# Moving the weight-conversion steps of an attention, experts and gate kernel off the expert changes

## The chip, the cores and the metric

The kernel runs on one core of one Trainium2 chip. The metric is the device time of one execution in microseconds. The core has five engines that run their own instruction queues in order: TensorE (PE, matmuls), VectorE (DVE), ScalarE (ACT), GpSimd (POOL) and SyncE (SP, which issues nearly all DMA transfers here). An engine that waits for a semaphore holds everything behind it in its queue.

## The reference

Banded attention, then a mixture of four experts, then a gated network whose output projection follows directly:

```python
x = attention(q, k, v)                       # (1536, 512)
p = domain_probs / (domain_probs.sum(-1, keepdims=True) + 1e-09)
for e in range(4):
    h = np.maximum(x @ w1[e], 0.0)           # (1536, 1024)
    out += p[:, e:e + 1] * (h @ w2[e])       # (1536, 512)
a = out @ moe2_w1
b = out @ moe2_w2
h = (a * b) @ w3
result = h @ w_out
```

The last four weights arrive as 64-bit floats. The kernel turns them into 32-bit floats itself, piece by piece, on the engines that are not TensorE.

## The kernel before

**Numbers.** Every float32 matrix is held as a sum of two parts, "h" and "l", and each product is three matmuls (`three`, lines 60 to 62: high by high, high by low, low by high). `split` (lines 54 and 55) makes the parts: ACT casts the high part, DVE or POOL subtracts to get the low one.

**Chunks and stages.** The 1536 tokens are three chunks of 512. After the attention, chunk 0 goes through all four experts alone: 32 items n = 0 to 31, each one hidden block of 128 rows (an "up" product) and, two items later, its share of the second product (a "down", 12 matmuls into the four PSUM tiles o0 to o3). Then chunks 1 and 2 go through the experts in reverse order in 16 pair steps n = 0 to 15, four for each expert. A pair step makes two hidden blocks for two chunks with seven half-size products instead of eight (Strassen's scheme, `Pairs.run`), whose sums are DVE additions from PSUM (line 735). The products share four PSUM tiles z. Pair steps 4, 8 and 12 change expert: they also run the last two downs of chunk 1 and all eight of chunk 2 of the expert before, in four lists `downs[0]` to `downs[3]` that stand between the products. At the end of a chunk's downs DVE multiplies o0 to o3 by the probabilities (line 836 for the first expert, 839 for later ones, after which POOL adds to `acc`, line 840), and the next down can't write o0 until DVE has read it. After pair step 15 the ten downs of the last expert follow ("the ends"), while the weights that the next stage needs are loaded and split into the slots. The gate stage then makes the product of the last two weights (`w34`, j = 0 to 7, each 24 matmuls) and after that the gate itself.

**The order of work** is written out by hand: `tc.manual_schedule` keeps every engine's queue in program order.

**Conversion steps.** `Convert.step` is called 43 times at places listed by hand. There are 40 pieces of 128 x 512. One step in the middle of the run does five things: ACT takes the absolute value of a piece that has landed (line 541) and POOL clamps it (line 543); SP stores the piece that the step before finished (line 571); DVE runs four instructions on the piece that the step before began (lines 550 to 553); POOL adds (line 554); and SP loads a further piece (line 580), which waits until DVE has read the buffer that it goes to. The 41st and 42nd step load nothing, and the 43rd call finds nothing to do. The places are `CONVERTS` (after item n of chunk 0), `INSIDE` (in pair step n, between the ACT relu and the DVE subtraction of one output), `BETWEEN` (in pair step n, list j, after its down m) and `ENDS` (after one of the ten last downs).

**Others that the change touches.** `XSUMS` are the items n of chunk 0 after which a part of the sums of x for the pair steps (t1 to t4) is made. `last_x(c, d)` (lines 844 and 845) turns a quarter of `acc[c]` into the high part on ACT and the low part on POOL; all twelve calls stand between the ends and the gate stage. The buffers of the conversion (`cpool`) are allocated behind those of the pair steps (`xp`, `tpool`) and given back with them before `w34` takes its place.

Of the kernel before, what the change touches and what calls it, by code (L numbers as in the profile page):

```python
# [27 lines left out]
KC, FC = DM // P, F // P  # L28
CW = 512
NCH = N // CW  # L30
# [5 lines left out]
FILL = (6, 4)  # L36
W_TILE = 4
LAG = 2
XSUMS = (21, 23, 24, 26, 27, 28)
CONVERTS = (4, 6, 7, 8, 10, 11, 12, 13, 14, 18, 20, 22)  # L40
ENDS = (2, 4, 6)
BETWEEN = [(4, 3, 0)] + [(n, j, m) for n in (4, 8, 12) for j, m in ((0, 0), (1, 0), (1, 1), (2, 0), (2, 1))]
INSIDE = [(n, 1, 1) for n in range(15) if n not in (4, 8, 12)]
BIG = 1.0e30
MASKED = -1.0e9

# [5 lines left out]
def split(nc, hi, lo, src, lo_engine=None):  # L52

    nc.scalar.copy(hi, src)  # L54
    (lo_engine or nc.vector).tensor_tensor(lo, src, hi.bitcast(F32), op=ALU.subtract)  # L55


def three(nc, out, wh, wl, xh, xl, start, stop):

    nc.tensor.matmul(out, wh, xh, start=start, stop=False)  # L60
    nc.tensor.matmul(out, wh, xl, start=False, stop=False)  # L61
    nc.tensor.matmul(out, wl, xh, start=False, stop=stop)  # L62
# [712 lines left out]
def experts_and_gate(tc, g, x_hi, x_lo, slots, experts, first_time):  # L775

    nc = tc.nc
    name = "" if first_time else "g"
    with ExitStack() as ctx:
# [2 lines left out]
        ps_z = ctx.enter_context(tc.tile_pool(name=name + "ps_z", bufs=4, space=PSUM))  # L782
        ps_a = ctx.enter_context(tc.tile_pool(name=name + "ps_a", bufs=1, space=PSUM))
        acc = [big.tile([P, KC, CW], F32, name=f"acc{c}") for c in range(NCH)]
        of_experts = ExitStack()
        xp = of_experts.enter_context(tc.tile_pool(name=name + "xp", bufs=1))
        tpool = of_experts.enter_context(tc.tile_pool(name=name + "xt", bufs=1))
        cpool = of_experts.enter_context(tc.tile_pool(name=name + "cv", bufs=2))
        ring = experts.ring
        if not first_time:  # L790
            for key in list(ring.of):
# [6 lines left out]
        def load_slot(s, src):  # L798

            raw = pool.tile([P, F], F32, name="wr")  # L800
            nc.sync.dma_start(raw, src)
            coming.append((s, raw))

        def land(keep=0):
            while len(coming) > keep:
                s, raw = coming.pop(0)
                split(nc, *slots[s], raw)

        work, pending = experts.work, experts.pending
        convert = Convert(nc, cpool, g.pieces if first_time else [])  # L810
# [5 lines left out]
        def down(e, c, f, fs=None, tail=False):  # L816
            fs = fs or list(range(FC))
            hi, lo = slots[f]
            hh, hl = pending.pop((e, c, f))
            if f == fs[0]:  # L820
                state["o"] = [
                    ps_z.tile([P, CW], F32, name="z") if tail else ps_a.tile([P, CW], F32, name=f"o{d}")
                    for d in range(KC)
                ]
            if f == fs[3]:
                state["p"] = xp.tile([P, CW], F32, name="prob")
                nc.sync.dma_start(state["p"], g.prob_dram[e, c * CW : (c + 1) * CW].partition_broadcast(P))
            o = state["o"]
            for d in range(KC):
                ds_ = slice(CW + d * P, CW + (d + 1) * P)  # L830
                three(nc, o[d], hi[:, ds_], lo[:, ds_], hh, hl, f == fs[0], f == fs[-1])
            ring.give((e, c, f))
            if f == fs[-1]:
                for d in range(KC):
                    if e == (pairs[0] if c else 0):
                        nc.vector.tensor_tensor(acc[c][:, d], o[d], state["p"], op=ALU.mult)
                        continue
                    t = tmp()
                    nc.vector.tensor_tensor(t, o[d], state["p"], op=ALU.mult)  # L839
                    nc.gpsimd.tensor_tensor(acc[c][:, d], acc[c][:, d], t, op=ALU.add)  # L840

        def last_x(c, d):

            nc.scalar.copy(x_hi[c][:, d], acc[c][:, d])
            nc.gpsimd.tensor_tensor(x_lo[c][:, d], acc[c][:, d], x_hi[c][:, d].bitcast(F32), op=ALU.subtract)
# [11 lines left out]
        def land_until(n):  # L857

            while coming and len(work) - len(todo) - len(coming) <= n:
                land(len(coming) - 1)  # L860
            load_more()
# [12 lines left out]
        for n, w in enumerate(work):  # L874
# [14 lines left out]
            if n >= LAG:  # L889
                e, c, f = work[n - LAG]  # L890
                down(e, c, f)
                if n >= FC and n % FC == LAG - 1:
                    land_until(n + FC - LAG - 1)
            if n in CONVERTS:
                convert.step()
            if n in XSUMS:
                next(xsums, None)
# [15 lines left out]
        for n in range(last + 1):  # L913
# [9 lines left out]
            def issue(j):  # L923
                for m, (e, c, f) in enumerate(downs[j]):
                    down(e, c, f, order.get(c))
                    if (n, j, m) in BETWEEN:
                        convert.step()
# [13 lines left out]
            def out(row, c, z):  # L941
# [6 lines left out]
                else:  # L948

                    to = x_hi[2][:, f - 4], x_lo[2][:, f - 4]  # L950
                experts.out((e, c, f), z, to, convert.step if (n, row, c) in INSIDE else None)

# [3 lines left out]
        for n, (e, c, f) in enumerate([w for d in ends(pairs[-1]) for w in d]):  # L956
            down(e, c, f, order[c], tail=c == 2)
            if n in ENDS:
                convert.step()
# [3 lines left out]
        split(nc, *slots[7], raws.here[0])  # L963
        raws.used()
        assert not raws.here
        for c in range(NCH):
            for d in range(KC):
                last_x(c, d)
        ring.free.remove((xp, "h3"))
        of_experts.close()  # L970

# [6 lines left out]
        for j in range(FC):  # L978
            hi, lo = slots[4 + j % 4]
            z = ps_z.tile([P, CW], F32, name="z") if j else ps_a.tile([P, CW], F32, name="o0")  # L980
            for gc in range(FC):
                oh, ol = slots[gc // 2]
                os_ = slice((gc % 2) * DM, (gc % 2 + 1) * DM)
                gs = slice(gc * P, (gc + 1) * P)
                three(nc, z, hi[:, gs], lo[:, gs], oh[:, os_], ol[:, os_], gc == 0, gc == FC - 1)
            split(nc, w34h[:, j], w34l[:, j], z)
            land()
            load_slot(4 + j % 4, g.w3t_f32[j + 4] if j < 4 else g.wab_f32[j - 4])

        def final(ps, hid, f, js, f0=0, f1=FC - 1):  # L990
            hh, hl = hid
            for j in js:
                ts = slice(j * P, (j + 1) * P)
                three(nc, ps[j], hh[:, ts], hl[:, ts], w34h[:, f], w34l[:, f], f == f0, f == f1)
# [226 lines left out]
def tile_attention_experts_gate(  # L1221
# [42 lines left out]
    slots += slot_tiles(rest, 4, FC)  # L1264

    experts_and_gate(tc, g, x_hi, x_lo, slots, experts, True)

    with tc.If(g.banded < 1):

        with tc.tile_pool(name="gn", bufs=1) as gn:  # L1270

            neg = gn.tile([P, 4], F32, name="neg")
            nc.vector.tensor_scalar(neg, wf, 0.0, 2.0**32, op0=ALU.is_lt, op1=ALU.mult)
            nc.vector.tensor_add(neg, neg, wf)
            full = gn.tile([P, 2], F32, name="full")
            for j in range(2):
                nc.vector.scalar_tensor_tensor(
                    full[:, j : j + 1], wf[:, 2 * j + 1 : 2 * j + 2], 2.0**32, neg[:, 2 * j : 2 * j + 1],
                    op0=ALU.mult, op1=ALU.add,
                )  # L1280

            nc.vector.tensor_scalar(full[:, 1:2], full[:, 1:2], -1024.0, None, op0=ALU.max)
            g.ng, g.nl = full[:, 0:1], full[:, 1:2]
            general_attention(tc, g, x_hi, x_lo)
        experts_and_gate(tc, g, x_hi, x_lo, slots, experts, False)
# [50 lines left out]
```

## Time and profile before

| | us |
|---|---|
| median of 3 runs | 832.39 |
| lowest and highest | 831.73, 832.85 |
| the profiled execution | 831.13 |
| its span, first to last instruction | 829.3 |
| PE busy in it | 805.5 (97%) |
| DVE, POOL, ACT busy | 615.0, 382.2, 315.0 |

The profile is one execution. Matmuls of 512 columns are shown 389 ns long but start one every 0.226 us where nothing holds them (46.00 us for 204 of them in a stretch without a wait), so a busy PE is a PE whose shown matmuls overlap. A row of the timeline ends with the idle time of the engine in front of the instruction and what ended it.

### The profile page before, as it was taken

What the parts mean: (1) busy time and instruction counts of PE and PEld (TensorE: products, weight loads), DVE (VectorE), ACT (ScalarE), POOL (GpSimd) and SP (SyncE); (2) the same over time, 40 slices, a digit from 0 to 9 for tenths busy, and PEclk for the clock granted to TensorE, in tenths of its full rate; (3) what the DMA queues carried; (4) which work ended last, traced back from release to release, by engine and by line L of the source; (5) the groups of instructions that cost most, each with busy time, mean ns of one, the idle gap of its engine ahead of it and who ended that gap; (6) DMA issues with size and microseconds to landing.
All of it is one profiled execution on the core that took longest, in us unless ns stands there. A gap on an engine that the chain in (4) does not pass through costs nothing.

```text
span 829.3 us, 11170 instructions
## 1 busy us (share of the span) xinstructions
PE 805.5 (97%) x3956; PEld 659.1 (79%) x3957; DVE 615.0 (74%) x1049; ACT 315.0 (38%) x655; POOL 382.2 (46%) x360
## 2 busy tenths in 40 slices
PE   9999999999999999899889989999999999999997
PEld 5888888888887887788677768778888888888886
DVE  8995477887829889889978988898553733888750
ACT  7996243443223342244313432333353332233210
POOL 7885032561336556554857567654291002433400
PEclk9999999999999999999999999999999999999999
DMA  9940456864202323433352344342532220201011
GB/s 274 278 123 12 151 197 208 252 187 159 71 26 64 114 94 125 163 100 117 114 202 80 113 127 148 93 134 69 171 127 97 81 72 26 97 32 51 2 44 62
DMA packets 42471, 96.52 MB, mean 116 GB/s; under 512 B 3930, under 2 KB 10122, under 8 KB 42406
## 3 DMA queue, kind: packets, MB, share of 16 engines
q1 hardware_dynamic: 41734, 95.18, 36.1%
q8 instruction: 33, 0.54, 0.3%
q10 hardware_dynamic: 672, 0.54, 0.3%
q14 instruction: 32, 0.26, 0.1%
HBM read 82.04 MB, written 13.66 MB: 115 GB/s over the span
## 4 chain that ended last, share of the span: by engine, by line
PE 64%; DVE 22%; ACT 4%; issue 4%; DMA 3%; POOL 2%; SPq 0%; DVEq 0%; ACTq 0%; POOLq 0%
PE z L60 13%; PE z L62 12%; PE z L61 12%; PE o L60 6%; PE o L62 6%; PE o L61 6%; DVE t L728 5%; DVE t L735 5%; PE sp L255 2%; DVE ca L551 2%; DVE cr L553 2%; DMA raw<-in_w_ab_dram 2%; DVE sl L55 2%; DVE ca L550 2%; PE tp L294 2%
## 5 line engine op out<-in xcount | busy, mean ns | idle before, releaser
L60 PE MATMUL z<-xh,sh 128*128 128x512 f32 x348 | 135.9, 391 | 1.4 <-DVE t L735 1.4
L62 PE MATMUL z<-xh,sl 128*128 128x512 f32 x348 | 135.5, 389 | 0.0
L61 PE MATMUL z<-xl,sh 128*128 128x512 f32 x348 | 135.5, 389 | 0.0
L543 POOL TENSOR_SCALAR ca<-ca 128x512 f32<-128x512 f32 x40 | 65.9, 1648 | 150.5 <-ACT ca L541 150.5
L55 POOL TENSOR_TENSOR sl<-wr,sh 128x512 fp32r<-128x512 f32 (+1 forms) x48 | 50.8, 1080 | 134.6 <-ACT sh L54 129.8
L55 DVE TENSOR_TENSOR sl<-wr,sh 128x1024 fp32r<-128x1024 f32 (+1 forms) x73 | 85.3, 1185 | 22.0 <-ACT sh L54 21.6
L54 ACT CAST sh<-wr 128x1024 fp32r<-128x1024 f32 (+2 forms) x121 | 87.0, 749 | 38.1 <-DMA wr<-in_w_moe_dram 13.7
L735 DVE TENSOR_TENSOR t<-t,z 128x512 f32<-128x512 f32 x112 | 74.7, 679 | 5.6 <-PE z L62 4.1
L60 PEld LDWEIGHTS z<-xh,sh 128*128 128x128 f32 x348 | 65.4, 188 | 16.6 <-issue 2.3
L62 PEld LDWEIGHTS z<-xh,sl 128*128 128x128 f32 x348 | 65.3, 188 | 14.3 <-DVE sl L55 0.2
L61 PEld LDWEIGHTS z<-xl,sh 128*128 128x128 f32 x348 | 65.3, 188 | 13.3
L840 POOL TENSOR_TENSOR acc<-acc,t 128x512 f32<-128x512 f32 x36 | 53.9, 1530 | 42.3 <-DVE t L839 42.3
L554 POOL TENSOR_TENSOR cr<-cr,ca 128x512 f32<-128x512 f32 x40 | 57.6, 1439 | 15.7 <-DVE cr L553 15.7
L55 POOL TENSOR_TENSOR sl<-t,sh 128x256 fp32r<-128x256 f32 (+1 forms) x48 | 53.0, 1119 | 20.6 <-ACT sh L54 20.2
L310 POOL TENSOR_TENSOR pt<-pt,r 128x232 f32<-128x232 f32 (+1 forms) x95 | 48.8, 546 | 7.6 <-DVE r L241 3.9
L541 ACT ACTIVATE ca<-raw 128x512 f32<-128x512 f32 x40 | 26.7, 668 | 63.1 <-DMA raw<-in_w_ab_dram 30.6
L60 PE MATMUL z<-sh,sh 128*128 128x512 f32 x120 | 46.7, 389 | 0.0
L61 PE MATMUL z<-sl,sh 128*128 128x512 f32 x120 | 46.7, 389 | 0.0
L62 PE MATMUL z<-sh,sl 128*128 128x512 f32 x120 | 46.7, 389 | 0.0
L281 ACT ACTIVATE pt<-t,negmax 128x232 f32<-128x232 f32 (+1 forms) x96 | 44.9, 475 | 4.0 <-DVE negmax L270 3.9
L54 ACT CAST sh<-t 128x256 fp32r<-128x256 f32 (+1 forms) x48 | 21.9, 478 | 54.4 <-DVE t L728 54.4
L624 ACT ACTIVATE xh<-t 128x512 fp32r<-128x512 f32 x24 | 15.2, 632 | 59.0 <-DVE t L735 59.0
(266 smaller groups left out, 1973.0 us busy)
## 6 DMA issues: line engine op xcount, KB each, us to landing
wr<-in_w_moe_dram SPq DMA_DIRECT2D x60, 512.0 KB, 3.6
raw<-in_w3t_dram SPq DMA_DIRECT2D x16, 512.0 KB, 4.3
raw<-in_w_ab_dram SPq DMA_DIRECT2D x16, 512.0 KB, 3.8
wr<-wab_d SPq DMA_DIRECT2D x16, 512.0 KB, 3.2
raw<-in_w_out_dram SPq DMA_DIRECT2D x8, 512.0 KB, 3.1
w3t_d<-cr SPq DMA_DIRECT2D x16, 256.0 KB, 2.4
wab_d<-cr SPq DMA_DIRECT2D x16, 256.0 KB, 4.1
wr<-w3t_d SPq DMA_DIRECT2D x8, 512.0 KB, 3.2
```

What stands on the lines that cost most here:

```text
L54: nc.scalar.copy(hi, src)
L55: (lo_engine or nc.vector).tensor_tensor(lo, src, hi.bitcast(F32), op=ALU.subtract)
L60: nc.tensor.matmul(out, wh, xh, start=start, stop=False)
L61: nc.tensor.matmul(out, wh, xl, start=False, stop=False)
L62: nc.tensor.matmul(out, wl, xh, start=False, stop=stop)
L281: nc.scalar.activation(st[u][gr][:, hh, 0:w], t[:, 0:w], AF.Exp, bias=nm, scale=-1.0, accum_out=st[u]["sums"][:, h : h + 1])
L310: nc.gpsimd.tensor_tensor(pt[:, hh, 0:w], pt[:, hh, 0:w], r[:, hh : hh + 1].to_broadcast([P, w]), op=ALU.mult)
L543: nc.gpsimd.tensor_scalar(a, a, 2.0**-15, None, op0=ALU.max)
L554: nc.gpsimd.tensor_tensor(rest, rest, a, op=ALU.add)
L728: nc.vector.tensor_tensor(out, a, b, op=op)
L735: add = lambda o, a, b: nc.vector.tensor_tensor(o, a, b, op=ALU.add)
L840: nc.gpsimd.tensor_tensor(acc[c][:, d], acc[c][:, d], t, op=ALU.add)
```

## The change

It moves conversion steps and spreads `last_x`. The number of calls stays 43, 42 of them with work.

- Chunk 0: three steps more, after items 24, 26 and 31; `XSUMS` goes from 21, 23, 24, 26, 27, 28 to 21, 23, 25, 27, 28, 29.
- Pair steps: none in pair step 0 (was one). At each expert change (pair steps 4, 8, 12) the step in list 0 and the second one in list 2 go: two less each time. Pair step 4 keeps the one in list 3.
- The ends: after downs 2 and 4 (was 2, 4 and 6, of which the last found nothing to do).
- The product `w34`: five calls, after j = 3 to 7, the last of which finds nothing to do.
- `cpool` is allocated ahead of `xp` and `tpool` and lives on through the gate stage.
- Of the twelve calls of `last_x` the four of chunk 0 stay in place; the other eight are spread over j = 0 to 6.

```diff
-XSUMS = (21, 23, 24, 26, 27, 28)
-CONVERTS = (4, 6, 7, 8, 10, 11, 12, 13, 14, 18, 20, 22)
-ENDS = (2, 4, 6)
-BETWEEN = [(4, 3, 0)] + [(n, j, m) for n in (4, 8, 12) for j, m in ((0, 0), (1, 0), (1, 1), (2, 0), (2, 1))]
-INSIDE = [(n, 1, 1) for n in range(15) if n not in (4, 8, 12)]
+XSUMS = (21, 23, 25, 27, 28, 29)
+CONVERTS = (4, 6, 7, 8, 10, 11, 12, 13, 14, 18, 20, 22, 24, 26, 31)
+W34 = (3, 4, 5, 6, 7)
+LASTX = ((0, 1), (2,), (3,), (4,), (5,), (6,), (7,), ())
+ENDS = (2, 4)
+BETWEEN = [(4, 3, 0)] + [(n, j, m) for n in (4, 8, 12) for j, m in ((1, 0), (1, 1), (2, 0))]
+INSIDE = [(n, 1, 1) for n in range(1, 15) if n % 4]
@@ experts_and_gate
+        cpool = ctx.enter_context(tc.tile_pool(name=name + "cv", bufs=2))
         of_experts = ExitStack()
         xp = of_experts.enter_context(tc.tile_pool(name=name + "xp", bufs=1))
         tpool = of_experts.enter_context(tc.tile_pool(name=name + "xt", bufs=1))
-        cpool = of_experts.enter_context(tc.tile_pool(name=name + "cv", bufs=2))
@@
-        for c in range(NCH):
-            for d in range(KC):
-                last_x(c, d)
+        for d in range(KC):
+            last_x(0, d)
@@ for j in range(FC)
             load_slot(4 + j % 4, g.w3t_f32[j + 4] if j < 4 else g.wab_f32[j - 4])
+            if j in W34:
+                convert.step()
+            for c in LASTX[j]:
+                last_x(1 + c // KC, c % KC)
```

## Rows read from the trace of the kernel before

**Rows 1.** The page, part 1: busy us (share of the span) and instructions of each engine.

```profile
PE 805.5 (97%) x3956; PEld 659.1 (79%) x3957; DVE 615.0 (74%) x1049; ACT 315.0 (38%) x655; POOL 382.2 (46%) x360
```

**Rows 2.** Waits of PE, 250 to 262 us: us in total, times, longest.

```profile
PE z L60 <- DVE t L735: 1.4, 2, 0.8
```

**Rows 3.** Waits of PE, 300 to 562 us, all of them.

```profile
PE o L60 <- DVE t L839: 7.2, 4, 2.4
PE o L60 <- DVE acc L836: 4.1, 2, 2.7
PE z L60 <- DVE t L735: 2.1, 4, 0.6
PE o L61 <- DVE h2l L627: 1.1, 1, 1.1
PE o L61 <- DVE h3l L627: 1.1, 1, 1.1
```

**Rows 4.** Windows: stretch, us, busy (instructions) by engine, PE clock, DMA share, GB/s.

```profile
300.00:560.00 260.00, 244.64 (x1061) 197.06 (x1059) 228.68 (x320) 85.82 (x162) 159.12 (x123) 1.00 0.39 127
596.00:642.00 46.00, 46.00 (x204) 38.10 (x204) 23.54 (x23) 20.43 (x30) 25.01 (x16) 1.00 0.37 120
```

**Rows 5.** Timeline of PE around its longest wait: start us, us, what.

```profile
344.37 0.39 PE L62 MATMUL z<-t2h,sl 128*128 128x512 f32 x1
347.48 0.47 PE L60 MATMUL o<-h2h,sh 128*128 128x512 f32 x1 [2.72 <-DVE acc L836]
347.78 0.39 PE L61 MATMUL o<-h2l,sh 128*128 128x512 f32 x1
```

**Rows 6.** Timeline of DVE, pair step 4, list 0.

```profile
311.18 1.42 DVE L550 TENSOR_SCALAR ca<-ca 128x512 int32<-128x512 int32 x1
...
314.53 0.69 DVE L553 SCALAR_TENSOR_TENSOR cr<-raw,cr 128x512 f32<-128x512 uint32 x1
315.14 2.48 DVE L836 TENSOR_TENSOR acc<-o,prob 128x512 f32<-128x512 f32 x4
```

**Rows 7.** Timelines of DVE and ACT, pair step 8, lists 2 and 3.

```profile
427.55 0.42 DVE L550 TENSOR_SCALAR ca<-ca 128x512 int32<-128x512 int32 x1
...
430.55 0.43 DVE L552 TENSOR_SCALAR cr<-ca 128x512 int32<-128x512 int32 x1 [0.88 <-DMA wab_d<-cr]
...
434.10 0.69 DVE L627 SCALAR_TENSOR_TENSOR h2l<-t,h2h 128x512 fp32r<-128x512 f32 x1 [1.80 <-ACT h2h L624]
...
432.88 0.66 ACT L541 ACTIVATE ca<-raw 128x512 f32<-128x512 f32 x1 [7.83 <-DMA raw<-in_w_ab_dram]
```

**Rows 8.** Timeline of DVE: the same addition in pair steps 5, 6 and 7.

```profile
361.26 0.68 DVE L735 TENSOR_TENSOR t<-t,z 128x512 f32<-128x512 f32 x1
...
377.23 0.68 DVE L735 TENSOR_TENSOR t<-t,z 128x512 f32<-128x512 f32 x1
...
393.20 0.68 DVE L735 TENSOR_TENSOR t<-t,z 128x512 f32<-128x512 f32 x1
```

**Rows 9.** Timeline of DVE ahead of pair step 0.

```profile
244.58 0.69 DVE L735 TENSOR_TENSOR t<-t,z 128x512 f32<-128x512 f32 x1 [4.13 <-PE z L62]
```

**Rows 10.** Timelines of SP's queue, DVE and PE, the ends and the first w34 products.

```profile
582.64 0.32 SPq L647 DMA_DIRECT2D wr<-wo_d  x1
...
587.60 0.37 SPq L647 DMA_DIRECT2D wr<-wo_d  x1
...
598.41 1.23 DVE L55 TENSOR_TENSOR sl<-wr,sh 128x1024 fp32r<-128x1024 f32 x1 [1.96 <-ACT sh L54]
...
601.03 0.39 PE L60 MATMUL z<-sh,sh 128*128 128x512 f32 x1
```

**Rows 11.** Timeline of DVE, w34 product j = 4 and the next.

```profile
624.56 1.84 DVE L55 TENSOR_TENSOR sl<-wr,sh 128x1024 fp32r<-128x1024 f32 x1 [0.25 <-ACT sh L54]
629.06 0.69 DVE L55 TENSOR_TENSOR w34l<-z,w34h 128x512 fp32r<-128x512 f32 x1 [2.65 <-ACT w34h L54]
```

**Rows 12.** The page, part 6: a load of the conversion, count, size, us to landing.

```profile
raw<-in_w_ab_dram SPq DMA_DIRECT2D x16, 512.0 KB, 3.8
```

## The prediction

> **What bounds the kernel now.** TensorE does: it is busy for 805.5 of 829.3 us [rows 1]. So the question is only where it isn't, and the first view is the list of its waits. Two waits, 1.4 us, lie in pair steps 0 and 1 [rows 2]. Between 300 and 562 us there are twelve, 7.2 + 4.1 + 2.1 + 1.1 + 1.1 = 15.6 us, and every one of them ends on a DVE instruction [rows 3]. Behind 562 us PE never waits; the stretch of the w34 products has it busy for 46.00 of 46.00 us [rows 4].
>
> A wait costs more than its length. The longest is shown as 2.72 us, but from the start of the matmul before it to that of the one behind it 347.48 - 344.37 = 3.11 us go by, where 46.00 / 204 = 0.2255 us is the pace [rows 4, 5]; the next start comes 0.30 us later. So the loss is 2.88 + 0.08 = 2.96 us, 0.24 more than the wait. I put 0.24 on each: the twelve lose 15.6 + 12 x 0.24 = 18.5 us. A second reading of the same stretch bounds that from above: its 1,061 matmuls needed 1,061 x 0.2255 = 239.3 of 260 us, so 20.7 us at most are lost, some of them matmuls whose records are missing [rows 4].
>
> The page "Perfetto Trace Analysis" of the Trainium skill ("Identifying the Most-Contended Engine") says that matmul busy time flatters TensorE and that the busy share of its weight loads shows the headroom. By that rule, 197.06 / 260 = 75.8% against 38.10 / 46 = 82.8% where nothing waits leaves 260 x (1 - 75.8 / 82.8) = 22.0 us and a time of 810.4 [rows 4]. The rows of the waits give 3.5 us less; I go by them, and the rule's time is rival F.
>
> DVE is late for two reasons, and a conversion step stands in both. First, at the expert changes. In list 0 of pair step 4 a step holds DVE from 311.18 to 315.14, 3.96 us, and the four readings of o0 to o3 stand right behind it, while PE wants o0 for the next down [rows 6]. In list 2 of pair step 8 the second of two steps begins at 427.55, waits 0.88 us for the store of the buffer that it writes, and its ACT part holds ACT until a load lands; the relu behind it comes late, DVE idles another 1.80 us for that, and only then come the readings of o [rows 7]. Six of the twelve waits are of this kind (11.3 us: three behind list 0, three behind list 3). Second, in the pair steps between. The same DVE addition starts at 361.26, 377.23 and 393.20, every 15.97 us [rows 8], while PE's 66 matmuls of a pair step need 66 x 0.2255 = 14.88. DVE falls 1.1 us behind in each, starts out late from the expert change, and by the third or fourth step PE waits for a z tile or for the low part of a hidden block. That makes the other six waits (4.3 us).
>
> **The change part by part.** (1) The step of list 0 goes at three changes. DVE then reads o0 to o3 right at 311.2 instead of 315.1, 3.9 us earlier, against a wait of 1.4 there: that wait goes, with 2.5 us to spare. Its siblings at the other changes are of the same make.
>
> (2) The second step of list 2 goes at three changes. In pair step 8, 427.55 to 431.6 is taken off DVE's queue, and the relu that waited behind the load is free of it, another 1.8 us [rows 7]: 5.9 us against a wait of at most 2.4. In pair step 4 the step of list 3 stays and takes some 4 us itself, but it too now stands 4 us earlier on DVE, against a wait of 2.7 [rows 3, 5]. So (1) and (2) give back 11.3 + 6 x 0.24 = 12.7 us.
>
> (3) The six waits of the pair steps: DVE comes out of each change earlier against PE, by at least the 2.5 us to spare, and gains up to 4. Three steps of 1.1 us eat 3.3 of that. In the old order the PE lost 4.3 + 6 x 0.24 = 5.7 us in two and a half expert rounds, some 2.3 a round, less than the 2.5 to 4. So these waits go as well: 5.7. Nearest to a doubt here: the margin is a microsecond or so, and the bound on the other side is that all 5.7 stay.
>
> (4) The step of pair step 0 goes. In DVE's queue it stands behind the additions that end the two waits of [rows 2] (the step belongs to the output (1, 1), made after them), so these stay (1.4 + 2 x 0.24 = 1.9 us) and nothing is gained; their cause is in the same queue (readings of o, then the sums of the weights), which the change leaves alone.
>
> (5) Three steps more in chunk 0. The one after item 31 falls on a DVE that idles 4.13 us before its next addition, the step takes 3.96 [rows 6, 9]. Those after items 24 and 26 take the place of a part of the sums of x, which moves on by an item. An item is 24 x 0.2255 = 5.4 us of PE, and its hidden block is due two items later, so 10.8 us of cover: cost 0. With the cover gone, one step, 4.0 us. A gain is excluded, since PE doesn't wait there. On SP each step's load waits for DVE, and behind it stand the first loads of the pair weights: these come up to 4 us later and are wanted a full item after that.
>
> (6) The ends. Two steps there now load (3.8 us each [rows 12]); before, none did. What stands behind them in SP's queue are the weights for the w34 products, and ACT's part of the second step waits for the load of the first, with the cast of slot 0 behind it. The tightest of these chains: the weights of the second w34 product are split by 598.41 + 1.23 = 599.64 and wanted at 601.03, 1.39 us of slack [rows 10]. On the other hand the third load of that chain went out at 587.60, 5 us behind the one before, held by the store of the very last piece [rows 10]; that store moves away. Bounds: 0, or one whole load late, 3.8 - 1.39 = 2.4. I take 0, as the loads before the slack are offset by that store.
>
> (7) The four working steps in w34 (j = 3 to 6; the call at j = 7 does nothing). DVE has 1.84 + 0.69 us of splits there in a product of 24 x 0.2255 = 5.4 [rows 11]. With 4.0 more it is 6.5, 1.1 late each, 4.4 in all; but what it splits is wanted three products later, 16.2 us. Cost 0. The eight spread calls of `last_x` run on ACT and POOL, and what they make is first read after the w34 products: cost 0, and the first casts of w34 lose eight casts ahead of them in ACT's queue, which nobody waited for: gain 0.
>
> (8) The kept buffers: `xp` and `tpool` hold what the w34 and gate tiles then overlay; `cpool` lay behind both and nothing reused it, so no wait arises: 0.
>
> Sum: 12.7 + 5.7 = 18.4, or 18.5 unrounded. The profiled execution's own time, 831.13, becomes 812.6 (its span 829.3 becomes 810.8, the 1.8 us around it stay). The median of the runs shown is 1.26 higher: 832.39 - 18.5 = 813.9.
>
> **The rivals.** A: the waits of the pair steps come back. For it: DVE's 15.97 against 14.88 stays as it is; against it: the head start of part (3). Time: 813.9 plus up to 5.7, say 817. B: the readings of o stay late at one or the other list because the steps that stay are slowed by loads and stores: the three waits behind list 3 stay, about half of 12.7, so 820.2. For it: even the steps that stay wait for loads; against it: 5.9 us off the queue for a wait of 2.4. C: the ends come 2.4 us late as in (6): 816.3. D: the steps do not matter, DVE is late through its other work, so nothing moves: 832. Against it: rows 6 show the step as the very instruction before the late one.
>
> E, slower than before: the four steps in w34 become a chain, each one's DVE part waiting for its predecessor's load. Place: ACT's in-order queue, where the absolute value waits for a load with the casts of w34 and of the slots behind it. Price at its worst: DVE 3.96, the longest that ACT stood for a load 7.83, its instruction 0.66 [rows 6, 7], the splits 2.53 [rows 11]: 15.0 a product, 9.6 over the 5.4, 38.4 in four, less the 16.2 of cover: 22.2 us, and 813.9 + 22.2 = 836.1. It decides from (18.5 + 16.2) / 4 + 5.4 = 14.1 us a product on. Against it: only two of the four steps load anything, and a step's DVE part works on the piece of the step before.
>
> One row speaks for E's direction: the same instruction took 1.42 us in rows 6 and 0.42 in rows 7. The Trainium skill's page "SBUF — State Buffer" ("Who interferes with whom") has a rule for it: DVE and GpSimd share a pair of ports, and the one that comes second stands still until the other's instruction is over. By it, steps that run beside the spread subtractions of POOL are dearer than those beside a quiet POOL; with 1.0 us on each of the four instructions, 4.0 a step, E's price without the wait for loads would be 4 x (10.5 - 5.4) = 20.4 against 16.2 of cover, 4.2 us, and a time of 818.1; that is rival G.
>
> F, more is lost than the waits show: PE's count of matmuls allows up to 20.7 us, so 811.7 without the waits of pair step 0; for it, that count; against it, records that are missing. By the page named above it would be 810.4.
>
> **How the numbers follow.** Forecast, 813.9: 0.66. A 0.12, B 0.06, C 0.05, D 0.03, E 0.04, F 0.02, G 0.02. Low: all of 20.7, 811.7, or the 1.9 of pair step 0 as well as the 18.5, 812.0; 811.5. High: all of A's 5.7, 819.6; that takes in C and G, and leaves out B, D and E, 0.13. A measurement here tells 0.2%, 1.7 us, from no change. Faster: forecast, A, B, C, F, G, 0.93; same: D, 0.03; slower: E, 0.04.
>
> **What would show it.** In the profile after: the list of PE's waits holds the two of pair steps 0 and 1 and at most one or two more; DVE's readings of o start within a microsecond of the last matmul into o at all three changes; the same addition in pair steps 5 to 7 comes nearer to 14.9 than to 15.97 us apart; PE stays busy throughout the ends, w34 and the gate. Waits on z tiles at the third pair step of a round would be A; on o behind list 3, B; a first wait at the second w34 product, C; waits in w34 from j = 7 on, E.

## The result, and the profile after

The changed kernel takes 811.79 us (median of 4 runs, 811.33 to 813.1) against 832.61 of the kernel before: a ratio of 0.9754, 95% interval 0.9737 to 0.9771. The forecast was 813.9, between 811.5 and 819.6.

| | before | after |
|---|---|---|
| profiled execution, us | 831.13 | 811.86 |
| span, us | 829.3 | 810.1 |
| PE busy, us | 805.5 (97%) | 802.1 (99%) |
| DVE, POOL, ACT busy, us | 615.0, 382.2, 315.0 | 614.9, 381.6, 315.5 |

The work of DVE, POOL and ACT is the same to within a microsecond; only where it stands has changed. PE's busy time is 3.4 us less, though it runs the same matmuls: a matmul behind a wait is shown longer (0.47 us in [rows 5], against 0.39), and late starts that are not listed as waits count as busy too. The page of after, part 1 (busy us and share of the span), and below it all waits of PE over the whole span of after (us in total, times, longest). Helper lines have moved down by two: L62 to L64 are the matmuls, L737 the additions, L838 and L841 the readings of o.

```profile
PE 802.1 (99%) x3957; PEld 661.3 (82%) x3957; DVE 614.9 (76%) x1049; ACT 315.5 (39%) x655; POOL 381.6 (47%) x360
```

```profile
PE z L62 <- DVE t L737: 1.4, 2, 0.8
PE tp L183 <- DVE warm L177: 1.2, 1, 1.2
```

The twelve waits of [rows 3] are gone, all of them, and the two of [rows 2] stand as they were. (The wait of 1.2 us is at the very start of both kernels.)

DVE in list 0 of pair step 4, after; [rows 6] are the same place before:

```profile
309.98 0.68 DVE L737 TENSOR_TENSOR t<-t,z 128x512 f32<-128x512 f32 x1
310.71 2.73 DVE L838 TENSOR_TENSOR acc<-o,prob 128x512 f32<-128x512 f32 x4
314.11 0.69 DVE L737 TENSOR_TENSOR t<-t,z 128x512 f32<-128x512 f32 x1 [0.67 <-PE z L64]
```

The four readings start at 310.71, where before they started at 315.14, and the next addition now waits 0.67 us for PE: the roles are exchanged. At the end of the same pair step the step of list 3 is still there, and the readings behind it start at 338.82 instead of 346.64. Against PE, DVE has gained 7 us there: PE's last matmul into o, 0.7 us behind the start of the readings now at 339.52, was 6.3 us ahead of it at 340.29. Before, then after:

```profile
346.64 2.48 DVE L836 TENSOR_TENSOR acc<-o,prob 128x512 f32<-128x512 f32 x4
```

```profile
338.21 0.69 DVE L555 SCALAR_TENSOR_TENSOR cr<-raw,cr 128x512 f32<-128x512 uint32 x1
338.82 2.48 DVE L838 TENSOR_TENSOR acc<-o,prob 128x512 f32<-128x512 f32 x4
```

The addition of [rows 8] in pair steps 5 and 6; in pair step 7 it starts at 386.85:

```profile
354.91 0.69 DVE L737 TENSOR_TENSOR t<-t,z 128x512 f32<-128x512 f32 x1 [0.42 <-PE z L64]
...
370.88 0.68 DVE L737 TENSOR_TENSOR t<-t,z 128x512 f32<-128x512 f32 x1
```

DVE still needs 15.97 us for a pair step, more than PE. It begins level with PE (the 0.42 us that it waits in pair step 5) and reaches the next expert change before its delay has cost PE anything.

Windows of after over the ends, the w34 products and the first gate steps (us, busy by engine, PE clock, DMA share, GB/s): PE busy without a break where the change put new work.

```profile
556.00:576.00 20.00, 20.00 (x90) 16.57 (x89) 12.82 (x13) 5.83 (x6) 9.40 (x7) 1.00 0.52 159
576.00:622.00 46.00, 46.00 (x205) 38.09 (x204) 34.95 (x37) 22.64 (x33) 33.18 (x21) 1.00 0.50 160
```

### The profile page after: what moved, and what is told of

The parts are those of the page before. It is cut to its first block, busy times and chain, and to the rows that moved or that the text cites. A ratio compares the mean times of both kernels' runs of the same rounds, so it can differ in the third digit from the quotient of the medians.

```text
span 810.1 us, 11165 instructions
## 1 busy us (share of the span) xinstructions
PE 802.1 (99%) x3957; PEld 661.3 (82%) x3957; DVE 614.9 (76%) x1049; ACT 315.5 (39%) x655; POOL 381.6 (47%) x360
## 4 chain that ended last, share of the span: by engine, by line
PE 95%; ACT 1%; DVE 1%; POOL 1%; DMA 1%; issue 0%; ACTq 0%; POOLq 0%; DVEq 0%
PE z L62 18%; PE z L64 18%; PE z L63 18%; PE o L62 12%; PE o L64 12%; PE o L63 12%; PE sp L257 2%; PE tp L296 2%; PE op L335 1%; PE op L336 1%; ACT pt L283 1%; PE sp L296 1%; DMA keys<-in_k_dram 1%; DVE t L730 1%; POOL pt L312 0%
## 5 line engine op out<-in xcount | busy, mean ns | idle before, releaser
L545 POOL TENSOR_SCALAR ca<-ca 128x512 f32<-128x512 f32 x40 | 68.2, 1706 | 155.2 <-ACT ca L543 155.2
L62 PE MATMUL z<-xh,sh 128*128 128x512 f32 x348 | 135.6, 390 | 1.4 <-DVE t L737 1.4
L64 PE MATMUL z<-xh,sl 128*128 128x512 f32 x348 | 135.5, 389 | 0.0
L57 DVE TENSOR_TENSOR sl<-wr,sh 128x1024 fp32r<-128x1024 f32 (+1 forms) x73 | 91.2, 1265 | 22.5 <-ACT sh L56 16.9
L737 DVE TENSOR_TENSOR t<-t,z 128x512 f32<-128x512 f32 x112 | 74.9, 680 | 10.2 <-PE z L64 8.7
L62 PEld LDWEIGHTS z<-xh,sh 128*128 128x128 f32 x348 | 65.3, 188 | 15.5 <-issue 1.2
L64 PEld LDWEIGHTS z<-xh,sl 128*128 128x128 f32 x348 | 65.3, 188 | 14.2 <-DVE sl L57 0.2
L842 POOL TENSOR_TENSOR acc<-acc,t 128x512 f32<-128x512 f32 x36 | 52.1, 1480 | 34.5 <-DVE t L841 34.5
L62 PE MATMUL z<-sh,sh 128*128 128x512 f32 x120 | 46.7, 389 | 0.0
L64 PE MATMUL z<-sh,sl 128*128 128x512 f32 x120 | 46.7, 389 | 0.0
```

What stands on the lines that cost most here:

```text
L545: nc.gpsimd.tensor_scalar(a, a, 2.0**-15, None, op0=ALU.max)
L737: add = lambda o, a, b: nc.vector.tensor_tensor(o, a, b, op=ALU.add)
```

## The experiments

Two theories. **P**, that of the prediction: a step costs what the reading or the deadline behind it on DVE comes late, so its place decides. **N**: what counts is the number of steps between the first and the last pair step, wherever in that stretch. All edits below are against the changed kernel, and "more than the changed kernel" compares with its median of 811.79. The kernel before, run again beside the experiments, had medians of 832.85 (the first three below and the sums of pair step 0) and 831.95 (the others), so less than a microsecond between two medians says nothing.

### The steps of list 0 back

```diff
-W34 = (3, 4, 5, 6, 7)
+W34 = (3, 4)
-... for j, m in ((1, 0), (1, 1), (2, 0))]
+... for j, m in ((0, 0), (1, 0), (1, 1), (2, 0))]
```

> The changed kernel with the step of list 0 put back at the three expert changes and three calls fewer in the w34 stage. Theory P (the place of a step counts: it costs what the readings of o behind it, or the next deadline on DVE, come late): the three waits behind list 0 come back, 4.7 us and 0.24 on each, 5.4 in all; DVE catches up in the rest of the change, so the waits of the pair steps do not come back: 811.8 + 5.4 = 817.2. Theory N (the number of steps between the first and the last pair step counts, wherever they stand): 20.8 us for seven steps moved out, 3.0 a step, so three steps give 811.8 + 9.0 = 820.8, the same as in e2_list2.

Measured: 815.58 us, ratio to the kernel before 0.9794 (0.9776 to 0.9812). Waits of PE beside the 1.4 us of pair steps 0 and 1:

```profile
PE o L62 <- DVE t L841: 2.8, 2, 1.6
...
PE o L63 <- DVE h3l L629: 0.5, 1, 0.5
```

3.8 us more than the changed kernel. Two waits behind list 0, not three: at the first expert change the step costs nothing, since DVE arrives there early enough (why, is read below from the run with the step in pair step 0). The pair steps stay almost free of waits (one of 0.5). P, at 817.2, is 1.6 too high; N, at 820.8, is off by 5.

### The second steps of list 2 back

```diff
-W34 = (3, 4, 5, 6, 7)
+W34 = (3, 4)
-... for j, m in ((1, 0), (1, 1), (2, 0))]
+... for j, m in ((1, 0), (1, 1), (2, 0), (2, 1))]
```

> The changed kernel with the second step of list 2 put back at the three expert changes and three calls fewer in the w34 stage. Theory P: the three waits behind list 3 come back (6.6 us and 0.24 on each, 7.3), and since DVE then leaves the change late, also the six waits of the pair steps (5.7): 811.8 + 13.0 = 824.8. Theory N: 820.8, as e1_list0.

Measured: 820.66 us, ratio 0.9853 (0.9835 to 0.9871), 8.9 us more than the changed kernel. Waits of PE:

```profile
PE z L62 <- DVE t L737: 3.5, 6, 0.8
PE o L62 <- DVE acc L838: 1.6, 1, 1.6
...
PE o L63 <- DVE h2l L629: 1.1, 1, 1.1
PE o L63 <- DVE h3l L629: 1.1, 1, 1.1
PE o L62 <- DVE t L841: 0.9, 1, 0.9
```

The six waits of the pair steps are all back: 3.5 less the 1.4 of pair step 0, and 1.1 twice, 4.3 us as before. Of the three behind list 3 two are back, smaller (1.6 and 0.9 against 2.7 and 2.4). The eight waits, 6.8 us and 0.24 on each, make 8.7 us; the medians lie 8.9 apart and the two profiled executions 10.3, so late starts that are not listed have a part here too. P's 824.8 is 4.1 too high, as one of its nine waits is missing and the two behind list 3 are small. The time falls on N's 820.8, but N wanted the same time for both experiments, and they lie 5.1 us apart with as many steps.

### Both back

```diff
-W34 = (3, 4, 5, 6, 7)
+W34 = ()
-... for j, m in ((1, 0), (1, 1), (2, 0))]
+... for j, m in ((0, 0), (1, 0), (1, 1), (2, 0), (2, 1))]
```

> The changed kernel with both steps put back at the three expert changes and none left in the w34 stage; only the steps of chunk 0 and of pair step 0, the buffers and the spread of last_x stay as changed. Theory P: all twelve waits, 18.5 us, 830.3. Theory N: six steps of 3.0, 829.8. If the steps of chunk 0, the buffers or the spread had given part of the gain, it would come out by that much lower.

Measured: 829.87 us, ratio 0.9964 (0.9951 to 0.9977), 18.1 us more than the changed kernel: most of the gain is given back. The time fits P (830.3) and N (829.8) alike. The two alone sum to 3.8 + 8.9 = 12.7. So the costs are not additive: each kind alone is partly paid from DVE's slack, both together are not. Of the 5.4 us between the two, some 1.5 in the trace are the clock (last section). Its waits of PE on o:

```profile
PE o L62 <- DVE t L841: 5.6, 4, 1.6
PE o L62 <- DVE acc L838: 4.1, 1, 4.1
...
PE o L63 <- DVE h3l L629: 1.1, 1, 1.1
```

In pair step 4 there was a wait of 1.36 us behind list 0 and one of 2.72 behind list 3 before, 4.08 in all [rows 3, 5]. Here the first is missing (DVE comes earlier, with no step in pair step 0; see the next experiment), and the second is 4.15: the lost time went to the next deadline on the same queue. With four waits on z tiles in the pair steps, 1.6 us, ten of the twelve waits are back, 12.4 of 15.6 us, and not all twelve, as P had it. This kernel is 3.0 us faster than the kernel before beside it (829.87 against 832.85), so that much of the gain does not hang on these six steps. What DVE has gained ahead of the first expert change is probably a part of it; the rest is not traced.

### The step after item 31 back in pair step 0

```diff
-CONVERTS = (..., 20, 22, 24, 26, 31)
-INSIDE = [(n, 1, 1) for n in range(1, 15) if n % 4]
+CONVERTS = (..., 20, 22, 24, 26)
+INSIDE = [(n, 1, 1) for n in range(15) if n % 4 or not n]
```

> The changed kernel with the step after item 31 of chunk 0 moved back into pair step 0. By part (4) of the prediction nothing comes of that step's place: the two waits of PE stay as they are (1.4 us) and the time is 811.8. Rival: the step in pair step 0 is what kept DVE late into the first expert change; then a wait of PE at list 0 or list 3 of pair step 4 shows, 1 to 3 us, up to 814.8.

Measured: 811.65 us, ratio 0.9757 (0.9741 to 0.9774). All waits of PE but that at the start of the program (1.2) and one of 0.4 on a load in the attention:

```profile
PE z L62 <- DVE t L737: 1.4, 2, 0.8
```

That step's place is worth nothing by itself, as part (4) had it. But it does move DVE: the readings in list 0 of pair step 4 start 0.2 us ahead of PE's last matmul into o with it (311.61 against 311.84) and 1.6 us without (310.71 against 312.32 in the changed kernel). Nothing waits for these 1.4 us here. But they fit the wait of 1.36 us at that place, which is there in the kernel before, with the step of pair step 0 and that of list 0, and missing in both experiments with that of list 0 alone.

### All of last_x back ahead of w34

```diff
-        for d in range(KC):
-            last_x(0, d)
+        for c in range(NCH):
+            for d in range(KC):
+                last_x(c, d)
@@ for j in range(FC)
-            for c in LASTX[j]:
-                last_x(1 + c // KC, c % KC)
```

> The changed kernel with all twelve calls of last_x back between the ends and the w34 stage. By part (7) of the prediction nothing waited for them: 811.8, no wait of PE behind 262 us. Rival: with the four conversion steps in the w34 stage the casts that stand ahead of the first w34 splits on ACT now matter, and PE waits for a z tile there: 8 casts of 0.52 us, up to 4.2 us more, 816.

Measured: 811.52 us, ratio 0.975 (0.9734 to 0.9767). Waits of PE beside those of pair step 0 and of the program's start:

```profile
PE z L62 <- DVE t L841: 0.3, 1, 0.3
```

One wait of 0.3 us shows at the second w34 product, on a z tile that DVE reads late. The time shows nothing of the spread.

### The sums of pair step 0 first

What is left are the two waits of pair steps 0 and 1. In the changed kernel DVE stands idle for 2.64 us there until the last down is done, then reads o four times, then makes the sums of the weights, and only then the additions for which PE waits. The edit uses the idle time for the sums, in pair step 0 alone:

```diff
         prep(0)
-        issue(0)
         early = n % (FC // 2) or not n
-        if early:
+        if not n:
+            prep(1)
+        issue(0)
+        if early and n:
             prep(1)
```

> The changed kernel with, in pair step 0 alone, the sums of the weights put ahead of the two downs and so ahead of the four readings of o in DVE's queue. If the two waits that are left come from DVE doing readings and sums one after the other behind the downs: DVE has 2.6 us idle there, the sums take some 4.7, so both waits (1.4 us, 1.9 with what lies around them) go or nearly go: 809.9 to 810.5, under both kernels. If they come from something else in that step (the slots that the splits write are still read by PE, and ACT and POOL wait in the middle of the sums' splits), the waits move to a later product and the time stays 811.8 or rises by what ACT stands still, up to 3 us.

Measured: 809.57 us, ratio 0.9726 (0.9709 to 0.9743), 2.2 us under the changed kernel and the fastest of all. DVE in the changed kernel, then in this one, then all waits of PE in this one but that of 1.2 us at the very start:

```profile
248.89 2.80 DVE L841 TENSOR_TENSOR t<-o,prob 128x512 f32<-128x512 f32 x4 [2.64 <-PE o L64]
...
256.16 0.68 DVE L737 TENSOR_TENSOR t<-t,z 128x512 f32<-128x512 f32 x1
```

```profile
245.68 1.37 DVE L730 TENSOR_TENSOR t<-wr 128x256 f32<-128x256 f32 x1
...
249.07 1.27 DVE L843 TENSOR_TENSOR t<-o,prob 128x512 f32<-128x512 f32 x2
...
252.18 0.68 DVE L737 TENSOR_TENSOR t<-t,z 128x512 f32<-128x512 f32 x1
```

```profile
PE sp L257 <- DMA keys<-in_k_dram: 0.6, 1, 0.6
```

The addition that PE waited for starts at 252.18; in the changed kernel at 256.16. Of the 2.3 us by which the two spans differ, 1.8 are gained here; the rest lies at the start of the program, where the edit does nothing. Behind the attention PE now waits for nothing.

### More steps in w34

Rival E put a point from which the steps in w34 would cost. Two experiments look for it. First, the three additional steps of chunk 0 out, seven calls in w34, all of them with work:

```diff
-CONVERTS = (..., 20, 22, 24, 26, 31)
-W34 = (3, 4, 5, 6, 7)
+CONVERTS = (..., 20, 22)
+W34 = (1, 2, 3, 4, 5, 6, 7)
```

> The changed kernel with the three additional steps of chunk 0 taken out and two more working steps in the w34 stage (seven calls, j = 1 to 7) so that more of them load. If the w34 stage has cover of three products for what its splits feed, 811.8 and no wait of PE there. Rival E of the prediction, a chain of load, ACT and DVE: PE waits in w34 or the gate, some 5 to 10 us.

Measured: 820.96 us, ratio 0.986 (0.9844 to 0.9876), 9.2 us more. Its waits of PE beside those of pair step 0 and of the program's start, and DVE's splits of the w34 products:

```profile
PE o L62 <- ACT h0h L56: 3.6, 1, 3.6
PE z L62 <- DVE w34l L57: 1.6, 1, 1.6
...
PE z L64 <- DVE sl L57: 0.8, 2, 0.4
```

```profile
598.21 0.68 DVE L57 TENSOR_TENSOR w34l<-z,w34h 128x512 fp32r<-128x512 f32 x1
604.52 0.68 DVE L57 TENSOR_TENSOR w34l<-z,w34h 128x512 fp32r<-128x512 f32 x1
611.02 0.69 DVE L57 TENSOR_TENSOR w34l<-z,w34h 128x512 fp32r<-128x512 f32 x1 [0.61 <-ACT w34h L56]
617.81 0.68 DVE L57 TENSOR_TENSOR w34l<-z,w34h 128x512 fp32r<-128x512 f32 x1
```

A product with a step takes DVE 6.3 to 6.8 us, about 1 more than PE's 5.4. It is not a chain of loads, since DVE waits less than 0.9 us for ACT in any product; the sum is that of part (7). But the steps are dear in part because of POOL. The first instruction of six of the seven steps takes 1.51 or 1.52 us instead of 0.41, and five of these end 0.3 us behind one of the spread subtractions of `last_x`, as here:

```profile
599.84 2.28 POOL L847 TENSOR_TENSOR xl<-acc,xh 128x512 fp32r<-128x512 f32 x1
...
600.88 1.51 DVE L552 TENSOR_SCALAR ca<-ca 128x512 int32<-128x512 int32 x1
```

In the changed kernel the last step takes DVE 2.25 us in all (620.18 to 622.43), with POOL idle meanwhile. No run has seven calls without the spread, so how much of the 9.2 us POOL's part makes stays open. And the cover is much smaller than I put it: PE waits as soon as the gate starts. Its 6.0 us of waits are not all of the 9.2; the clock has a part (last section). The first weights of the gate are split in the changed kernel by 610.99 + 1.92 = 612.91 and first used at 619.91, 7.0 us later; in this kernel that split ends at 620.35, behind the first use at 619.39. The split and the first use in the changed kernel:

```profile
610.99 1.92 DVE L57 TENSOR_TENSOR sl<-wr,sh 128x1024 fp32r<-128x1024 f32 x1 [0.15 <-ACT sh L56]
```

```profile
619.91 0.39 PE L62 MATMUL z<-xh,sh 128*128 128x512 f32 x1
```

Second, two steps in each of the eight products and none at the expert changes:

```diff
-CONVERTS = (..., 20, 22, 24, 26, 31)
-BETWEEN = [(4, 3, 0)] + [...]
+CONVERTS = (..., 20, 22, 24)
+BETWEEN = []
@@ for j in range(FC)
-            if j in W34:
-                convert.step()
+            convert.step()
+            convert.step()
```

> Two steps in each of the eight w34 products (sixteen), none at the expert changes, 13 in chunk 0. It asks where the cover of that stage ends. If a step costs DVE 4.0 us there, two and the splits are 10.5 us against 5.4 of PE: 41 us late in all, less 16.2 of cover, PE waits some 25 us, 836. If it costs 2.5, 7.5 against 5.4: 17 us late, the cover all but holds, 811 to 813. If loads chain, since the second step of a product takes up a load that the first has only just sent (3.8 us to landing), ACT stands each time and with it the casts: 9 to 10 us a product, some 15 to 20 us of waits, 827 to 832.

Measured: 868.38 us, ratio 1.0433 (1.0413 to 1.0453), 56.6 us more than the changed kernel and worse than any of the three cases. Its waits of PE from w34 on, one of the waits of ACT for a load, and a window of that stretch:

```profile
PE z L62 <- ACT sh L56: 17.5, 6, 3.7
PE z L64 <- DVE sl L57: 6.3, 6, 1.2
PE o L62 <- ACT h0h L56: 6.1, 1, 6.1
PE z L62 <- DVE w34l L57: 4.8, 1, 4.8
```

```profile
611.30 0.66 ACT L543 ACTIVATE ca<-raw 128x512 f32<-128x512 f32 x1 [8.65 <-DMA raw<-in_w_ab_dram]
```

```profile
600.00:612.00 12.00, 8.99 (x24) 6.35 (x24) 9.68 (x10) 2.60 (x5) 8.48 (x6) 0.72 0.48 174
```

24 matmuls, one product, in 12 us. Half of the 34.7 us of waits end on an ACT cast of slot weights, and ACT stands for a load in front of it, as the third case (loads chain through ACT's queue) had it; its price, 15 to 20 us, was too low. The rest is mostly the clock, whose granted share is 0.72 in this window (below).

## Why the prediction was right, point by point

**The bound and the loss.** PE's waits between 300 and 562 us were put at 18.5 us, 15.6 and 0.24 for each of the twelve. The profiled executions lie 831.13 - 811.86 = 19.3 apart, but that is not the gain of the stretch, because the one of after lost 0.9 us at the very start, where the two kernels do the same. PE there, before and after:

```profile
6.52 1.47 PE L181 MATMUL tp<-warm 128*128 128x512 bf16 x6
```

```profile
7.43 1.47 PE L183 MATMUL tp<-warm 128*128 128x512 bf16 x6
```

Up to pair step 0 the same work stands 0.9 us later in after (its addition at 256.16 against 255.23), and at the gate 19.2 earlier (its first matmul at 619.91 against 639.12). So 20.1 us were gained between. The starts behind the twelve waits, matched one by one, make 18.5 of them, so the 0.24 was good; the other 1.6 are in starts that came 0.2 us late or less and that no wait shows. That term the sum left out. The median came 2.1 us lower than forecast, nearly all of it for three reasons: the 1.6, less the 0.9 of the start, which hid more than half of it by chance, and the 1.26 by which the profiled execution of before lay under its median; that of after lies on its own, so the 1.26 should not have been carried over (the last section has a probable reason).

**Parts (1) to (3), which step pays for which wait.** The mechanism holds; the allotment of the parts does not. I gave list 0 three waits (5.4 us with what lies around them), list 2 another three and the pair steps as a third heading. Put back alone, list 0 costs 3.8 us and list 2 costs 8.9, and 5.4 us belong to neither alone. What failed is the allotment of 12.7 to parts (1) and (2) and 5.7 to part (3) as a sum of separate parts: the queue has one slack, and whichever step is left uses it up first. For the forecast it made no difference, as both were removed. The sign given for it came: at all six places DVE starts reading o before PE's last matmul into o starts, by 0.7 to 1.6 us.

**Part (3), the head start.** Right in its effect, with all six waits gone, and in its cause: with the late step of list 2 back, the same six waits, 4.3 us, are back. But what I named as its mark was wrong. I wrote that the additions of pair steps 5 to 7 would come nearer to 14.9 us apart. They are 15.97 apart as before, and on the working of part (3) itself they had to be: DVE falls behind by 1.1 us a step and only starts from further ahead.

**Part (4).** Right on the two waits, which stayed at 1.4 us and didn't care where that step stands; that nothing is gained seems to hold only where the step of list 0 is gone as well, as read at the experiment with that step. The cause it named, readings of o and then the sums of the weights, is shown by the experiment that puts the sums first.

**Part (5).** Right: no wait of PE in chunk 0, before or after.

**Part (6).** Right in time: no wait at the ends. In after the split for the second w34 product runs from 579.30 to 580.53 and its first use is at 581.83, so the slack is 1.30 us, where it was 1.39. Rival C had little room left.

**Part (7).** Cost 0, as forecast, but with a mis-sized term. DVE's 6.5 us a product was a little high: the splits of the changed kernel come 5.75 to 6.3 apart. The cover was put at 16.2 us, three products; in the changed kernel 7.0 are left, and in the kernel before there were 639.12 - 631.23 = 7.9. The reason is the order of the program: the split of the gate's first weights stands behind that of product j = 5, which can't start before this product is done (ACT's cast for it starts at 628.43 in the kernel before), and only two products follow. So lateness in this stage costs from far lower than the 14.1 us a product of rival E: seven working steps, three more than the changed kernel has there, cost 9.2 us. E had been priced as unlikely for the wrong reason.

The splits of after from which that follows, and one case of DVE and POOL meeting in this stage; 639.12 and 631.23 are read in the same way from the trace of before:

```profile
604.41 0.69 DVE L57 TENSOR_TENSOR w34l<-z,w34h 128x512 fp32r<-128x512 f32 x1 [0.43 <-ACT w34h L56]
610.16 0.68 DVE L57 TENSOR_TENSOR w34l<-z,w34h 128x512 fp32r<-128x512 f32 x1
616.46 0.68 DVE L57 TENSOR_TENSOR w34l<-z,w34h 128x512 fp32r<-128x512 f32 x1
...
611.79 2.27 POOL L847 TENSOR_TENSOR xl<-acc,xh 128x512 fp32r<-128x512 f32 x1
...
612.83 1.51 DVE L552 TENSOR_SCALAR ca<-ca 128x512 int32<-128x512 int32 x1
```

POOL's subtraction ends at 611.79 + 2.27 = 614.06, and DVE's instruction, which takes 0.41 to 0.42 us alone, ends at 614.34, 0.28 later. That is how the Trainium skill's page "SBUF — State Buffer" ("Who interferes with whom") tells it: the one that comes second stands still until the other is done. The trace agrees here. Rival G was built on that rule. It did not come about in the changed kernel, where the four steps start with 0.83, 0.41, 1.51 and 0.41 us and one of them alone met POOL in full; but its cover of 16.2 us was wrong too, and in the run with seven calls six of the seven steps met this delay.

**Part (8).** No wait arose from the kept buffers.

**The rivals.** A, B, C, D, E and G did not come about in the changed kernel. A is what the second experiment shows when DVE leaves the change late. F, more lost than the waits show, came about for the most part: 20.1 us of its 20.7, against 18.5. It had been given a chance of 0.02, and its time of 811.7 is nearer to the 811.79 than the forecast, in part by luck: it too carries the 1.26 over, and the 0.9 of the start is in neither. The 22.0 us that the prediction sets beside it are 1.9 too many.

## What to carry to other kernels

Filler work on a queue in program order costs nothing where the queue arrives early, and where a reading that another engine waits for stands right behind it, it costs what that reading comes late; look at the instruction in front of the late one, not at the engine's busy share. Take such work out at all the places of one slack, since a single one left can use the slack up, and before moving it measure the cover of the new place from the end of the split or load to its first use, not from the number of loop turns between them. When nearly all waits are gone, look for idle time of the same engine just ahead of the ones that are left: here there were 2.64 us, and a reordering by a few lines filled them. Before trusting one profiled execution, hold it against the other executions: here one lay 1.3 us under its median and the other lost 0.9 us at the start of the program.

## What the runs showed of the hardware that was not expected

A long wait of PE can cost more than itself, when the granted clock falls. With both steps back, PE waited 4.15 us; about a microsecond after it started again the granted share fell to 0.5, the lower of the two levels (1.2 GHz), and the matmuls came 0.43 us apart instead of 0.23. PE's timeline and windows (the value behind POOL's busy time is the clock) in that kernel:

```profile
347.69 0.47 PE L62 MATMUL o<-h2h,sh 128*128 128x512 f32 x1 [4.15 <-DVE acc L838]
...
349.42 0.63 PE L62 MATMUL o<-h2h,sh 128*128 128x512 f32 x1
...
350.28 0.63 PE L64 MATMUL o<-h2h,sl 128*128 128x512 f32 x1
```

```profile
349.00:352.00 3.00, 3.00 (x9) 2.32 (x8) 2.31 (x5) 1.93 (x4) 0.34 (x1) 0.50 0.17 67
```

Seven matmuls start in these 3 us (the row also counts two that only reach into it), where thirteen would at 0.2255 us: 1.4 us or so on top of the wait. With seven steps in w34 the lower level was there as well when PE started again after its wait of 3.6 us, at 637.33, and lasted until about 643:

```profile
636.00:640.00 4.00, 2.67 (x6) 2.13 (x7) 3.06 (x5) 2.05 (x3) 1.26 (x1) 0.55 0.41 141
```

With two steps in each w34 product the waits came back every few microseconds and the granted share stayed near 0.7. That kernel lost 56.6 us where its listed waits are 34.7; 90 of its matmuls start in stretches at the lower level, and at 0.2 us more for each that makes 18 us of the difference (an estimate).

The waits of 2.72 us and less in the kernel before left the clock at 1.00 in the profiled execution [rows 4, 5]. That execution is not typical of the kernel. Of 19 others of the same kernel that were timed beside the experiments, 16 had a mean granted clock of 0.990 to 0.996, where the profiled one had 0.999; the four of the changed kernel had 0.999. So in most executions the kernel before also ran some microseconds at the lower level, which would explain why the profiled one lay under its median, and a part of the 20.8 us between the medians would be the clock. Where it fell, no trace shows.
